# A gated attention kernel on one Trainium2 core: block order, tail priorities, filler matmuls and the last adds

## The chip, the core and the metric

The kernel runs on one core of one Trainium2 chip. A core has a matrix engine (TensorE, PE in the profile), a vector engine (VectorE, DVE), an engine for activation functions (ScalarE, ACT), a general engine (GpSimd, POOL) and a queue processor (SyncE, SP) that here only issues DMAs. They work on an on-chip memory (SBUF) and on a small memory for matmul results (PSUM, eight banks of 128 x 512 fp32). The engines run independently, each through its own list of instructions in order, and wait for each other with semaphores.

The metric is the time of one execution on the device in microseconds (us). Before the change the median of three runs is 483.76 us (483.73 to 483.79).

## What is computed

```
xn  = layernorm(x)                              # x: 2048 x 448
q, k, v = split(xn @ wqkv)                      # 16 heads of 28
o   = softmax(q k^T / sqrt(28)) v               # per head, 2048 x 2048 scores
s   = o @ wo
g   = silu(gelu(xn @ w1 + b1) @ w2 + b2)        # hidden size 1792
out = x + s * g
```

All tensors are bf16. The exponentials of the softmax, 16 x 2048 x 2048 of them, are the largest single piece of elementwise work.

## The kernel before

**Tiles and blocks.** The 16 heads form four groups g of four, since four heads of 28 (padded to 32) fill the 128 rows of the matrix engine. The 2048 queries form four chunks c of 512. A pair (g, c) is a block; there are 16. A block has 64 score tiles (16 key tiles x 4 heads), each 128 keys x 512 queries, one PSUM bank. All 1024 tiles are numbered m, and m // 64 is the block's number b. In the kernel before, g = b // 4 and c = b % 4: all chunks of a group are run before the next group, and the last four blocks are (3,0), (3,1), (3,2), (3,3).

**The stream.** Units of three tiles run through six PSUM banks, the ring: TensorE computes scores (`p_scores`, L1129), ScalarE takes the exponential of the unit into one of 21 SBUF slots P (`p_exps`, L1160), TensorE multiplies P by v (`p_pv`, L1346) and accumulates in one bank, `acc`. One column of v holds a constant, so that `acc` also holds the softmax's sums.

**Late tiles.** Some tiles are not given to ScalarE. VectorE copies the scores as integers out of the ring (L1183, L1274) and takes the exponential by a polynomial, one or two tiles at a time (`p_exp2`, L1297 to L1304). `pick_late` decides tile by tile, by VectorE's planned backlog against two values per block, THS and SLACKS.

**The end of a block.** VectorE copies `acc` to SBUF (E_sb, L1403), after which the next block's PV may begin. TensorE collects the sums (L1410), VectorE takes reciprocals (L1413), GpSimd splits them into two bf16 parts (L1415, L1416), TensorE spreads them (L1425), VectorE multiplies (L1432). The result overwrites this block's part of q.

**The last block** is cut by queries into pieces of 256, 128 and 128, so that its ends can overlap: E copies at L1377, sums spread by one matmul with `selb` (L1388), a reciprocal on 128 x 128 (L1391), and the product (L1394).

**Gate and output.** Between the score units the matrix engine computes the two layers of the gate branch: GELU on ScalarE in the middle of the run, the second layer at L1065, its bias at L1070, SiLU through a tanh on ScalarE (L1080) and VectorE (L1083). `p_out` and `p_last` make 128 x 448 output tiles: matmuls with wo (`t_wo`, L1442), times g (L1451), plus x (L1453), then a DMA from SP (L1459, for the last chunk L1457). A tile of chunk c needs all four groups of that chunk, and the gate of that chunk. For the very last tile (chunk 3, tile 3), tanh waits for the last exponential (L1093) and GpSimd forms g in two steps (L1095, L1097). While the blocks run, one PSUM bank (`misc`) is left for all of this; two ring banks' worth comes free with the last two exponentials.

**Who sets the order.** The program is planned as it is built. Every piece of work is a small process that hands out tasks with an engine, what they read and write, an estimated duration and a priority (a smaller number goes first). `run` repeatedly takes the task that can start first; among those of one engine that could start within 0.1 us of it, the one of the smallest priority. The order that comes out is fixed in each engine's instruction list. Estimated times never reach the chip; only order and waits do.

**Fillers.** [...]`p_busy` (L857) emits groups of three small matmuls of a zero matrix into `acc` (priority 95) whenever the planned busy share of the last 3.4 us is low (`pe_low`, from the history `pe_hist`). They add zero to `acc`, so they are ordered with its readers and writers.

## Time and profile before

| | |
|---|---|
| median of three runs | 483.76 us |
| the profiled execution, its own time | 484.9 us |
| its span, first to last instruction | 483.1 us |
| mean granted TensorE clock | 0.993 |
| exponentials on ScalarE (L1160) | 350 instructions: 249 of three tiles, 100 of two, 1 of one |
| late tiles on VectorE | 68 (L1183) and 8 (L1274) |
| starts of the 15 E copies (L1403) | 47.1 (block 0) ... 259.8, 315.2, 343.9, 371.6, 401.0, 424.3, 453.0 (block 14) |
| second gate layer's bias steps (L1070), last | 414.5 |
| output tiles' products (L1451) | 420.4 to 479.9 |
| last exponential ends | 476.46 |
| output DMAs, median from issue to landing | 1.9 us (six of 224 KB), 1.7 us (four of 112 KB) |

How to read it: shares and durations are of one execution. A line number names the line of the kernel, or of the helper, that issued the instruction. "Idle before" is the time in which an engine waited, with the instruction that ended the wait. In windows and the timeline, times count from the span's start. Between an engine's last instruction and the end of the span lies the last output DMA.

### The profile page before, as it was taken

To read this page: it belongs to the slowest core of one execution; us is meant where nothing else is said; L and a number is where in the kernel's file an instruction comes from. 1 tells how busy PE (TensorE), PEld (TensorE's weight loads), DVE (VectorE), ACT (ScalarE), POOL (GpSimd) and SP (SyncE) were. 2 spreads that over 40 slices of the span, in tenths; PEclk is the share of its full clock that TensorE was granted. 3 is DMA by queue.
4 is the path that set the end of the run, shared out by engine and by line. 5 is a ranking of instruction groups with operands and counts; after the bars stand their busy time and mean duration, and the time that the engine had idled before them with its cause. 6 is when DMAs were issued, how large, how long until landed. Compare 5 with 4: busy or idle time off the path is not lost.

```text
span 483.1 us, 10155 instructions
## 1 busy us (share of the span) xinstructions
PE 438.5 (91%) x4232; PEld 168.1 (35%) x4268; DVE 407.6 (84%) x592; ACT 468.8 (97%) x390; POOL 43.2 (9%) x77
## 2 busy tenths in 40 slices
PE   6999899998889898999989988999999999999995
PEld 5442333332223333332323343333333333333453
DVE  8946888989978989989878749899997999889785
ACT  5999999999999999999999999999999999999994
POOL 7470000000010000000101000010100100100001
PEclk9998999999999999999999999999999999999998
DMA  8501000000000000000400000000101010011011
GB/s 247 149 9 28 1 0 2 1 2 2 0 1 1 1 1 1 1 2 1 134 1 0 1 2 0 1 2 1 38 1 40 1 38 1 23 37 58 3 39 39
DMA packets 8288, 11.08 MB, mean 23 GB/s; under 512 B 1650, under 2 KB 6898, under 8 KB 8243
## 3 DMA queue, kind: packets, MB, share of 16 engines
q1 hardware_dynamic: 8098, 10.21, 7.0%
q8 instruction: 33, 0.54, 0.5%
q10 hardware_dynamic: 144, 0.23, 0.1%
q14 instruction: 13, 0.10, 0.1%
HBM read 8.61 MB, written 1.84 MB: 22 GB/s over the span
## 4 chain that ended last, share of the span: by engine, by line
ACT 45%; PE 32%; issue 17%; DVE 5%; ACTq 0%; DVEq 0%
ACT P L1160 42%; PE ring L1129 9%; PE acc L1346 6%; PE misc L1065 4%; PE acc L857 3%; PE misc L695 2%; ACT h L1044 2%; PE misc L1007 1%; PE acc L839 1%; PE misc L949 1%; PE misc L1442 1%; PE ring L1007 1%; ACT w L1080 1%; PE ring L949 1%; DVE kT L1298 0%
## 5 line engine op out<-in xcount | busy, mean ns | idle before, releaser
L1160 ACT ACTIVATE P<-ring 128x1536 bf16<-128x1536 f32 (+1 forms) x350 | 428.9, 1469 | 1.7 <-PE ring L1129 1.5
L1129 PE MATMUL ring<-qT,kT 32*128 32x512 bf16 (+2 forms) x1144 | 136.5, 360 | 26.1 <-ACT P L1160 22.0
L1346 PE MATMUL acc<-P,vaug 128*32 128x512 bf16 (+2 forms) x1074 | 95.0, 363 | 1.0 <-issue 0.5
L1129 PEld LDWEIGHTS ring<-qT,kT 32*128 32x128 bf16 x1144 | 35.5, 91 | 132.8 <-ACT P L1160 123.5
L1183 DVE TENSOR_SCALAR x_sb<-ring 128x512 int32<-128x512 f32 x68 | 46.8, 688 | 14.2 <-PE ring L1129 13.0
L1065 PE MATMUL misc<-w,h 128*128 128x448 bf16 x224 | 52.3, 355 | 0.1
L1415 POOL CAST rhi<-rc 128x16 bf16<-128x16 f32 x15 | 10.3, 686 | 402.5 <-DVE rc L1413 255.6
L857 PE MATMUL acc<-ident,zero 128*128 128x128 bf16 x516 | 44.8, 221 | 0.0
L1346 PEld LDWEIGHTS acc<-P,vaug 128*32 128x32 bf16 x1074 | 24.4, 93 | 51.0 <-issue 46.6
L857 PEld LDWEIGHTS acc<-ident,zero 128*128 128x128 bf16 x516 | 29.8, 98 | 21.3 <-issue 19.4
L1007 PE MATMUL misc<-xnT,w 128*128 128x512 bf16 x127 | 35.9, 382 | 1.3 <-issue 0.8
L990 DVE CAST h<-misc 128x512 bf16<-128x512 f32 x35 | 24.1, 688 | 8.1 <-PE misc L1007 7.0
L1304 DVE SCALAR_TENSOR_TENSOR x_sb<-x_sb,kT 128x1024 uint16<-128x1024 int32 (+1 forms) x24 | 26.7, 1111 | 0.5
L1302 DVE SCALAR_TENSOR_TENSOR kT<-kT 128x1024 f32<-128x1024 f32 (+1 forms) x24 | 26.6, 1110 | 0.5
L1298 DVE SCALAR_TENSOR_TENSOR kT<-kT 128x1024 f32<-128x1024 f32 (+1 forms) x24 | 26.5, 1104 | 0.6
L1300 DVE SCALAR_TENSOR_TENSOR kT<-kT 128x1024 f32<-128x1024 f32 (+1 forms) x24 | 26.4, 1102 | 0.2
L1065 PEld LDWEIGHTS misc<-w,h 128*128 128x128 bf16 x224 | 17.3, 97 | 23.9 <-issue 12.1
L1007 PE MATMUL ring<-xnT,w 128*128 128x512 bf16 x82 | 19.3, 380 | 2.0 <-ACT h L1044 1.6
L1298 DVE SCALAR_TENSOR_TENSOR w<-w 128x1024 f32<-128x1024 f32 (+1 forms) x18 | 20.3, 1128 | 0.3
L1304 DVE SCALAR_TENSOR_TENSOR x_sb<-x_sb,w 128x1024 uint16<-128x1024 int32 (+1 forms) x18 | 20.3, 1130 | 0.2
L1300 DVE SCALAR_TENSOR_TENSOR w<-w 128x1024 f32<-128x1024 f32 (+1 forms) x18 | 20.3, 1130 | 0.2
L1302 DVE SCALAR_TENSOR_TENSOR w<-w 128x1024 f32<-128x1024 f32 (+1 forms) x18 | 20.3, 1129 | 0.1
(154 smaller groups left out, 449.6 us busy)
## 6 DMA issues: line engine op xcount, KB each, us to landing
h<-in_A_x_dram SPq DMA_DIRECT2D x4, 448.0 KB, 3.3
w<-in_B_w_dram SPq DMA_DIRECT2D x1, 1568.0 KB, 7.3
x_sb<-in_A_x_dram SPq DMA_DIRECT2D x3, 448.0 KB, 5.2
w<-in_B_w_dram SPq DMA_DIRECT2D x1, 1344.0 KB, 9.4
out_dram<-h SPq DMA_DIRECT2D x6, 224.0 KB, 1.9
h<-in_A_wqkv_dram SPq DMA_DIRECT2D x3, 168.0 KB, 5.5
out_dram<-h SPq DMA_DIRECT2D x4, 112.0 KB, 1.7
wo<-in_A_wo_dram SPq DMA_DIRECT2D x16, 24.5 KB
```

What stands on the lines that cost most here:

```text
L857: ins = eng.matmul(K.acc[:, 0:128], K.zero[:, :], K.ident[:, :], start=False, stop=True, skip_group_check=True)
L990: yield _Task(DVE, lambda eng: eng.tensor_copy(dst, bank), [tok], wr, 0.69, 0.0, 2)
L1007: ins = eng.matmul(bank, K.w1[:, kt, ft * 128:(ft + 1) * 128], K.xnT[:, kt, c * 512:(c + 1) * 512], start=(kt == 0), stop=(kt == KT - 1))
L1065: ins = eng.matmul(ps, hv[:, ft, t * 128:(t + 1) * 128], K.w2[:, ft, :], start=(ft == 0), stop=(ft == FT - 1))
L1129: return eng.matmul(K.ring[:, RB[m], col:col + nq], K.kT[32 * j:32 * j + 32, g, t * 128:(t + 1) * 128], K.qT[32 * j:32 * j + 32, g, c * 51 ...
L1160: return eng.activation(K.P[:, p0:p0 + n, :], K.ring[:, b0:b0 + n, :], ACTF.Exp, scale=SM_SCALE)
L1183: yield _Task(DVE, lambda eng, m=m, i=i, half=half: eng.tensor_scalar(K.ysb[i][:, 512 * half:512 * half + 512], K.ring[:, RB[m], :], SM_SC ...
L1298: yield _Task(DVE, lambda eng: eng.scalar_tensor_tensor(u, v, EXP_A, v, op0=ALU.add, op1=ALU.mult), [tv], [tu], d1, 0.0, 4)
L1300: yield _Task(DVE, lambda eng: eng.scalar_tensor_tensor(u, u, EXP_B, u, op0=ALU.add, op1=ALU.mult), [tu], [tu], d1, 0.0, 4)
L1302: yield _Task(DVE, lambda eng: eng.scalar_tensor_tensor(u, v, EXP_D, u, op0=ALU.mult, op1=ALU.add), [tv, tu], [tu], d1, 0.0, 4)
L1304: yield _Task(DVE, lambda eng: eng.scalar_tensor_tensor(pl.bitcast(dt.uint16), y, 2.0 ** -9, u, op0=ALU.mult, op1=ALU.add), ty + [tu], [K. ...
L1346: return eng.matmul(K.acc[32 * j:32 * j + 32, q0:q0 + nq], K.vaug[:, t, 4 * g + j, :], ap[:, col:col + nq], tile_position=(0, 32 * j), sta ...
```

## The change

- **Block order.** A table GC gives (g, c) for each block number. The first eleven are as before; then come (3,0), (3,1), (3,2), (2,3), (3,3). So the last two blocks both belong to chunk 3, and chunks 0 to 2 have all four groups one block earlier.
- **Late-tile values.** THS changes for blocks 11 (8 to 7), 13 (8 to 4) and 14 (7 to 9), SLACKS for block 8 (3 to 2).
- **No fillers ahead of a PV copy.** A flag `hold` is set when a block's last PV matmuls have been planned and cleared when the E copy has been; while it is set, tasks of priority 90 or more on TensorE are no candidates.
- **The history of activity** counts the sums' small matmuls (L877, L1410) with a weight of 0.15 or 0.3.
- **Look-ahead in the end.** From the last 18 tiles on, TensorE and VectorE give up the chosen task for one of smaller priority number that can start before the chosen one would have ended less 0.1 us.
- **Priorities in the end.** The last tile's steps get priority 0 (1 for its last wo matmul), and tiles 0 to 2 of the last chunk a 2 for the `selb` matmul. The first three wo matmuls of a last-chunk tile become three tasks.
- **x added by GpSimd.** The adds of L1453 move to GpSimd for output tiles 8 to 13 of 16 (all of chunk 2, tiles 0 and 1 of chunk 3).
- **The last gate tile.** Its add (L1097) moves from GpSimd to VectorE.

```diff
+GC = [(b // C, b % C) for b in range(11)] + [(3, 0), (3, 1), (3, 2), (2, 3), (3, 3)]
...
-THS = (8.0, 4.0, 7.0, 8.0, 4.0, 7.0, 9.0, 6.0, 6.0, 8.0, 8.0, 8.0, 8.0, 8.0, 7.0, 3.0)
-SLACKS = (6.0, 5.0, 3.0, 5.0, 2.0, 6.5, 9.0, 6.5, 3.0, 4.0, 7.0, 6.0, 8.0, 6.0, 8.0, 3.0)
+THS = (8.0, 4.0, 7.0, 8.0, 4.0, 7.0, 9.0, 6.0, 6.0, 8.0, 8.0, 7.0, 8.0, 4.0, 9.0, 3.0)
+SLACKS = (6.0, 5.0, 3.0, 5.0, 2.0, 6.5, 9.0, 6.5, 2.0, 4.0, 7.0, 6.0, 8.0, 6.0, 8.0, 3.0)
...
+TAIL = 18
+POOL_ADD = 8
...
-            self.pe_hist.append((start, start + t.dur))
+            self.pe_hist.append((start, start + t.dur * t.w))
...
-                    if s is not None:
+                    if s is not None and not (self.hold and p[3].E == PE and p[3].prio >= 90):
                         cand.append((s, p))
...
+            if self.exp_m >= MTOT - TAIL and E in (PE, DVE):
+                for s2, p2 in sorted(((c[0], c[1]) for c in cand), key=lambda c: c[0]):
+                    if p2[3].E == E and p2[3].prio < p[3].prio and s2 < s + p[3].dur - 0.1:
+                        s, p = s2, p2
+                        break
...
             yield _Task(ACT, lambda eng: eng.activation(sg[:, 3, :], fb[:, 3, :], ACTF.Tanh, scale=0.5),
-                        [K.b_fsb[c % 2]], [K.b_sig3], 0.47, 0.0, 0)
+                        [K.b_fsb[c % 2]], [K.b_sig3], 0.87, 0.0, 0)
             yield _Task(POOL, lambda eng: eng.tensor_tensor(o, sg[:, 3, :], fb[:, 3, :], ALU.mult),
-                        [K.b_sig3, K.b_fsb[c % 2]], [K.b_h[c], K.b_g3], 0.85, 0.05, 0)
-            yield _Task(POOL, lambda eng: eng.tensor_tensor(o, o, fb[:, 3, :], ALU.add),
-                        [K.b_fsb[c % 2]], [K.b_h[c], K.b_g3], 0.85, 0.05, 0)
+                        [K.b_sig3, K.b_fsb[c % 2]], [K.b_h[c], K.b_g3m], 1.03, 0.05, 0)
+            yield _Task(DVE, lambda eng: eng.tensor_tensor(o, o, fb[:, 3, :], ALU.add),
+                        [K.b_fsb[c % 2], K.b_g3m], [K.b_h[c], K.b_g3], 0.4, 0.0, 0)
...
             if end:
+                K.hold = True
                 K.spawn(K.p_epi(b) if b < NBLK - 1 else K.p_epi4(first - NBLK + 1), 0.5)
...
         K.E_done = NBLK - 1 + s
+        K.hold = False
...
-        yield _Task(DVE, lambda eng: eng.tensor_tensor(o, o, K.x2[:, c, t, :], ALU.add),
-                    [K.b_x2[c], wr], [wr], 0.4, 0.0, 3)
+        E, dur = (POOL, 1.05) if POOL_ADD <= 4 * c + t < 14 else (DVE, 0.4)
+        yield _Task(E, lambda eng: eng.tensor_tensor(o, o, K.x2[:, c, t, :], ALU.add),
+                    [K.b_x2[c], wr], [wr], dur, 0.0, pr)
...
-        bank, tok = yield ("bank", lambda: K.on_done[(G - 1) * C + c] and K.g_done[c])
+        bank, tok = yield ("bank", lambda: K.on_done[GC.index((G - 1, c))] and K.g_done[c])
...
-        yield K.t_wo(ps, tok, c, t, (0, 1, 2), 3)
+        for g in range(G - 1):
+            yield K.t_wo(ps, tok, c, t, (g,), 3)
         yield ("until", lambda: K.on4[t])
-        yield K.t_wo(ps, tok, c, t, (3,), 3)
+        yield K.t_wo(ps, tok, c, t, (3,), 3 if t < 3 else 1)
```

Left out: the same lookup of (g, c) in `p_scores`, `p_mlate`, `p_pv` and `p_epi`, the new field w of a task, and the priorities named above.

## The prediction

> **What bounds the kernel now.** I read the page first (engine shares, costliest groups), then the chain of work in order of time, the waits, a table of windows by block, and last the timeline of the end.
>
> The page:
>
> ```profile
> PE 438.5 (91%) x4232; PEld 168.1 (35%) x4268; DVE 407.6 (84%) x592; ACT 468.8 (97%) x390; POOL 43.2 (9%) x77
> ...
> L1160 ACT ACTIVATE P<-ring 128x1536 bf16<-128x1536 f32 (+1 forms) x350 | 428.9, 1469 | 1.7 <-PE ring L1129 1.5
> ...
> L1183 DVE TENSOR_SCALAR x_sb<-ring 128x512 int32<-128x512 f32 x68 | 46.8, 688 | 14.2 <-PE ring L1129 13.0
> ```
>
> ScalarE is the bound: the softmax exponentials (L1160) run almost without a gap. The 68 tiles of L1183, and 8 more of L1274, are the "late" ones that VectorE exponentiates. What a tile costs ScalarE is read from the chain in order of time (start, length, what):
>
> ```profile
> 367.67 0.82 ACT P L1160
> 368.58 1.10 ACT P L1160
> 369.91 2.53 ACT P L1160 x2
> ```
>
> An instruction of two tiles holds ScalarE 0.91 us (to 368.58), one of three 1.33 (to 369.91): 0.42 per tile. One more late tile is worth 0.42 us as long as VectorE can pay for it. Against 0.91 and 1.33, the excess spacing over all exponentials after the first block is about 4.2 us, about 2.0 of that within half a microsecond of a block's end.
>
> The table of windows for the last two blocks and the end:
>
> ```profile
> core 0: us, PE busy (x) PEld busy (x) DVE busy (x) ACT busy (x) POOL busy (x), PEclk, DMA share, GB/s
> ...
> 424.30:453.00 28.70, 26.65 (x301) 11.52 (x304) 24.02 (x36) 28.70 (x24) 0.41 (x2) 1.00 0.10 34
> 453.00:476.50 23.50, 21.81 (x458) 11.72 (x452) 18.41 (x34) 23.50 (x20) 0.95 (x2) 1.00 0.08 27
> 476.50:483.10 6.60, 1.89 (x24) 0.73 (x22) 3.86 (x8) 0.42 (x1) 2.06 (x2) 0.77 0.16 52
> ```
>
> ScalarE is full until the last exponential, then 6.6 us follow in which one chain runs. VectorE is idle for 4.7 us of block 14 and 5.1 of block 15. The waits name one item that the change addresses, the copy of the PV bank (total, times, longest):
>
> ```profile
> DVE E_sb L1403 <- PE acc L857: 4.1, 5, 2.1
> ```
>
> **What the Trainium skill says.** (1) SBUF — State Buffer, "Who interferes with whom": a VectorE instruction with two SBUF inputs contends with a GpSimd instruction that reads SBUF, and "the second one to issue" (its summary's words) blocks until the first ends. The trace agrees both ways:
>
> ```profile
> 237.20 1.18 DVE L1298 SCALAR_TENSOR_TENSOR kT<-kT 128x1024 f32<-128x1024 f32 x1
> ...
> 237.35 1.08 POOL L1415 CAST rhi<-rc 128x16 bf16<-128x16 f32 x1 [23.19 <-DVE rc L1413]
> ...
> 156.34 0.20 POOL L1415 CAST rhi<-rc 128x16 bf16<-128x16 f32 x1 [21.90 <-DVE rc L1413]
> ```
>
> A GpSimd cast of 0.20 us takes 1.08 beside a VectorE step of a late tile and ends 0.05 after it. In the other direction, VectorE's L657 at 6.9 us took 1.00 us instead of 0.38 while GpSimd's L726 (6.78 to 7.78) ran. (2) TensorE: Matmul & The Clock Gate, "Architectural detail": VectorE's queue is strictly in order, so what stands behind a waiting copy waits too; the trace shows VectorE idle for up to 2.1 us before L1403. (3) The same page, Part 1: the clock falls only after about 3.4 us of low activity. The trace shows 1.00 in the blocks and 0.77 in the end stretch; holding fillers back for half a microsecond should not lower it.
>
> **The change part by part.**
>
> *No filler ahead of the PV copy.* Block 14's last PV matmuls end at 452.51, fillers (L857) on the same bank run to 452.96, the copy starts at 452.99: 0.42 us late. Block ends read in this way give 0.53, 0.53, 0.40, 0.25 and 0.42, 2.1 us in all, and nothing at the other ten. PE's next PV and its sums wait for that copy; ScalarE does not, since the 21 P slots (seven exponentials of three) cover it. So the gain is VectorE time, 1.07 us in the last three blocks. If fillers were needed for the clock, the loss would show as PEclk under 1.00. Weighting the tiny matmuls in the filler history adds fillers of 0.17 us; I cost them at nothing because PE waits for ScalarE 123.5 us in all at L1129.
>
> *The block order.* (3,2) now ends as block 13 (424.3), not 14 (453.0), so chunk 2's four output tiles are released some 29 us earlier. In the trace they lie at 458.8 to 467.5, between the steps of block 15's two late tiles: 4 x (0.62 + 0.39) = 4.05 us of VectorE. The late result that PV of block 15's first half waits for ends at 465.2. One more late tile alone costs 0.69 + 0.41 + 4 x 0.69 = 3.86 us, so the freed time pays for one: -0.42. Group 3's projections, wanted a block earlier, end at 311.3, before block 11 starts (343.9): no cost. The four tiles go into block 14 behind those of chunks 0 and 1 (they last ran 437.0 to 444.9, 2.4 us apart, so to about 455): 4 x 0.62 = 2.5 us of L1451 there at most; its 4.7 us of idle covers that. Their two output DMAs move with them on SP's queue, which then holds nothing else; they land in 1.9 us.
>
> *Thresholds.* A lower value of block 13 (8 to 4) admits fewer late tiles, a higher one of block 14 (7 to 9) more; blocks 8 and 11 move by one. No row prices this: between two tiles fewer and two more, +0.85 to -0.85.
>
> *x added by GpSimd.* Six adds of 0.39 leave VectorE, four of them (1.56 us) in block 14; the last two are in the end stretch, where VectorE has room. GpSimd takes 1.03 us for this shape (L1097) and is otherwise idle there. But the adds have two SBUF inputs, and so have the four steps of a late tile: each can hold VectorE up for 0 to 1.03 us. Four adds give back 1.56 and cost 0 to 4.1; I take half, 2.1, so half a microsecond net loss to VectorE, and +0.15 us for ScalarE where a late copy (L1183) is delayed and its ring bank comes free late (bounds 0 and +1.9).
>
> *One more late tile from the rest.* VectorE gets back 1.07 (holds) + 1.56 (adds) in blocks 12 to 14, against 3.47 per tile in a pair (0.69 + half of 0.69 + 4 x 1.22). That is 0.76 of a tile: -0.32.
>
> *Block-end gaps of ScalarE.* 2.0 us now, mostly a late copy and an E copy close together. An earlier E copy and changed late positions may mend or make such gaps: -0.6 to +0.6, I take -0.25.
>
> *The end.*
>
> ```profile
> 477.16 0.29 DVE L1377 CAST E_sb<-acc 128x128 bf16<-128x128 f32 x1 [0.27 <-PE acc L1346]
> 477.44 0.63 DVE L1451 TENSOR_TENSOR h<-ring,h 128x448 bf16<-128x448 f32 x1
> ...
> 477.81 0.22 PE L1388 MATMUL ring<-E_sb,selb 128*128 128x128 bf16 x1
> 478.06 0.96 DVE L1391 RECIPROCAL w<-ring 128x128 f32<-128x128 f32 x1
> 478.11 1.03 POOL L1097 TENSOR_TENSOR h<-h,w 128x448 bf16<-128x448 bf16 x1
> 479.13 0.29 DVE L1394 TENSOR_TENSOR qT<-E_sb,w 128x128 bf16<-128x128 bf16 x1
> ```
>
> The sum matmul L1388 stands behind output matmuls on PE, and the reciprocal behind tile 2's L1451 on VectorE. In the undisturbed case of 467.18 the reciprocal starts 0.33 us after the copy's end (467.51); here 0.61 (477.45 to 478.06). Priority and look-ahead can give back 0.28. The GpSimd add L1097 becomes a VectorE add of 0.39, which has its place in the 0.46 us between L1394 and L1451 (479.42 to 479.88), where tile 2's add is now. So tile 2's two instructions must go earlier or come last: bounds -0.35 and +0.73 (1.01 - 0.28). I take -0.28, since without chunk 2's work block 15's first half, and with it tiles 0 to 2, can be over earlier.
>
> Sum: -0.42 - 0.32 - 0.25 + 0.15 - 0.28 = -1.1 us. Of the profiled execution (484.9, its span 483.1 and 1.8 around it) that makes 483.8. It stands 1.1 above the median of 483.76, and the same step from the median gives 482.6.
>
> **Rivals.** *A late tile gained and one lost*: block 14 is fuller by up to 2.5 us, block 13 admits fewer, so the count stays at 68, and the tail and half a gap remain: -0.4, 483.3. For it: the last blocks' VectorE idle time is only 4.7 and 5.1 us. Against it: block 15's room is freed where a late tile can use it.
>
> *Slower, the shared port*: in block 14 VectorE is busy 24.0, plus 2.5 of moved work, minus 0 (those adds were not there before), plus up to 4.1 of blocking: 30.6 us in a block of 28.7. From 2.2 us of blocking on (4.7 - 2.5) VectorE overruns, late copies hold ring banks, and ScalarE waits for PE. At the full 4.1 that is +1.9; with a late tile's worth lost too and the tail gained, 483.76 + 1.9 - 0.28 = 485.4 at most, and some 485.1 typically. For it: the two lock cases above. Against it: L1451 comes straight before each add, and VectorE's next step starts within 0.04 us, ahead of GpSimd, which then waits.
>
> *Tile 2 last*: the look-ahead prefers everything of tile 3, and tile 2's L1451 and L1453 close the kernel: +0.73 at the end, minus one late tile: 484.1.
>
> **How the numbers follow.** 0.2% is 0.97 us, about what a measurement can tell: faster is under 482.79, slower over 484.73. The main case, 482.6 (its own range 481.2 to 482.8: two late tiles more below, half the tail gain missing above), gets 0.54; the unchanged count 0.22, all within the bound; tile 2 last 0.10, of it 0.03 slower; the port 0.14, of it 0.13 slower. So faster 0.54, same 0.30, slower 0.16. The range 481.2 to 484.4 leaves out the port case and a twentieth below.
>
> **What would show it.** L1160's tiles fewer by one or two and the late copies 69 or 70; chunk 2's L1451 before 456 us; no filler between the last PV and the E copy; the reciprocal 0.33 us after the last copy; about 6.3 us after the last exponential. Wrong would be: late copies at 68 or fewer, VectorE steps of late tiles lengthened by GpSimd's adds, ScalarE waiting for PE L1129 for more than the present 1.5 us, or tile 2's add as the last instruction.

## The result, and the profile after

The changed kernel takes 486.71 us (median of four runs, 485.87 to 487.63) against 483.75 (483.66 to 483.79) before: a ratio of 1.0062, 95% interval 1.0044 to 1.008. It is slower by 3.0 us and lies outside the predicted range, which ended at 484.4.

The page of the changed kernel: engine shares, and the groups that answer to L1160 and L1183 of before (now L1169 and L1192), with TensorE's P times v (L1355):

```profile
PE 438.1 (90%) x4223; PEld 168.0 (35%) x4259; DVE 403.3 (83%) x576; ACT 469.7 (97%) x390; POOL 49.1 (10%) x82
...
L1169 ACT ACTIVATE P<-ring 128x1536 bf16<-128x1536 f32 (+1 forms) x350 | 429.6, 1465 | 3.1 <-PE ring L1138 2.7
...
L1355 PE MATMUL acc<-P,vaug 128*32 128x512 bf16 (+2 forms) x1075 | 95.0, 363 | 3.0 <-DVE x_sb L1313 1.8
...
L1192 DVE TENSOR_SCALAR x_sb<-ring 128x512 int32<-128x512 f32 x67 | 46.1, 688 | 13.4 <-PE ring L1138 12.5
```

ScalarE is still the bound, but three things differ: one late tile fewer (67, was 68), ScalarE waits 2.7 us for scores (1.5 before), and a new wait stands before L1355: TensorE waits 1.8 us for the last step of a late tile (L1313). The table of windows around the end of block 14 and for the end stretch:

```profile
core 0: us, PE busy (x) PEld busy (x) DVE busy (x) ACT busy (x) POOL busy (x), PEclk, DMA share, GB/s
...
452.00:455.00 3.00, 1.20 (x18) 0.41 (x22) 2.44 (x4) 1.74 (x3) 0.00 (x0) 1.00 0.23 82
455.00:458.00 3.00, 3.00 (x53) 1.45 (x57) 0.86 (x2) 2.93 (x3) 0.41 (x2) 0.65 0.00 0
458.00:461.00 3.00, 3.00 (x70) 1.66 (x60) 2.86 (x5) 2.08 (x3) 0.00 (x0) 0.78 0.01 3
```

In the first window TensorE (PE) works 1.20 of 3 us and ScalarE 1.74; in the next two TensorE is full, but at 0.65 and 0.78 of its clock, and ScalarE loses time again in the third. Most of the loss sits in these nine microseconds, of which ScalarE idles 2.25; the end stretch itself became shorter (6.14 us from the last exponential's end, 6.61 before).

**Where the time went.** The exponentials run back to back, so I count their *excess*: the spacing of two starts less 0.90 us after an instruction of two tiles and less 1.33 after one of three, summed by block. One tile moved to or from ScalarE counts 0.43 (1.33 less 0.90). Against before:

| term | us |
|---|---|
| one late tile fewer (67 against 68) | +0.43 |
| excess in block 14: 2.00 against 0.02 | +1.98 |
| excess in block 15: 1.26 against 0.26 | +1.00 |
| excess in block 12: 0.56 against 0.15 | +0.41 |
| excess in block 11 | -0.27 |
| end stretch: 6.14 against 6.61 | -0.47 |
| sum | +3.08 |

The medians differ by 2.96. The profiled execution of before holds 1.25 us in its first block that no other profile but that of e11 holds, with the clock at 0.65 from 42 to 46 us. It is left out of the table. Because of it the two spans (483.08 and 484.89) differ by only 1.81, less than the medians.

### The profile page after: what moved, and what is told of

Same layout as the page of the kernel before. It is cut to its first block, busy times and chain, and to the rows that moved or that the text cites. A ratio compares the mean times of both kernels' runs of the same rounds, so it can differ in the third digit from the quotient of the medians.

```text
span 484.9 us, 10132 instructions
## 1 busy us (share of the span) xinstructions
PE 438.1 (90%) x4223; PEld 168.0 (35%) x4259; DVE 403.3 (83%) x576; ACT 469.7 (97%) x390; POOL 49.1 (10%) x82
## 4 chain that ended last, share of the span: by engine, by line
ACT 42%; PE 31%; issue 17%; DVE 8%; DMA 1%; POOL 0%; ACTq 0%; DVEq 0%; POOLq 0%
ACT P L1169 39%; PE ring L1138 9%; PE misc L1074 6%; PE acc L1355 6%; PE acc L866 2%; ACT h L1053 2%; PE misc L1016 1%; PE misc L704 1%; ACT w L1089 1%; DVE x_sb L1313 1%; DVE st L632 1%; PE misc L1454 1%; PE misc L958 1%; PE ring L1016 1%; DVE kT L1311 1%
## 5 line engine op out<-in xcount | busy, mean ns | idle before, releaser
L1169 ACT ACTIVATE P<-ring 128x1536 bf16<-128x1536 f32 (+1 forms) x350 | 429.6, 1465 | 3.1 <-PE ring L1138 2.7
L1138 PE MATMUL ring<-qT,kT 32*128 32x512 bf16 (+2 forms) x1144 | 136.6, 361 | 26.2 <-ACT P L1169 22.5
L1355 PE MATMUL acc<-P,vaug 128*32 128x512 bf16 (+2 forms) x1075 | 95.0, 363 | 3.0 <-DVE x_sb L1313 1.8
L1138 PEld LDWEIGHTS ring<-qT,kT 32*128 32x128 bf16 x1144 | 35.5, 91 | 133.1 <-ACT P L1169 120.6
L1192 DVE TENSOR_SCALAR x_sb<-ring 128x512 int32<-128x512 f32 x67 | 46.1, 688 | 13.4 <-PE ring L1138 12.5
L1355 PEld LDWEIGHTS acc<-P,vaug 128*32 128x32 bf16 x1075 | 24.4, 94 | 51.5 <-issue 44.6
L1311 DVE SCALAR_TENSOR_TENSOR kT<-kT 128x1024 f32<-128x1024 f32 (+1 forms) x22 | 26.5, 1204 | 0.4
L1309 DVE SCALAR_TENSOR_TENSOR kT<-kT 128x1024 f32<-128x1024 f32 (+1 forms) x22 | 26.4, 1200 | 0.3
L1307 DVE SCALAR_TENSOR_TENSOR kT<-kT 128x1024 f32<-128x1024 f32 (+1 forms) x22 | 25.6, 1165 | 0.5
L1313 DVE SCALAR_TENSOR_TENSOR x_sb<-x_sb,kT 128x1024 uint16<-128x1024 int32 (+1 forms) x22 | 25.7, 1168 | 0.3
L1307 DVE SCALAR_TENSOR_TENSOR w<-w 128x1024 f32<-128x1024 f32 (+1 forms) x18 | 20.3, 1128 | 0.3
L1313 DVE SCALAR_TENSOR_TENSOR x_sb<-x_sb,w 128x1024 uint16<-128x1024 int32 (+1 forms) x18 | 20.3, 1130 | 0.2
L1309 DVE SCALAR_TENSOR_TENSOR w<-w 128x1024 f32<-128x1024 f32 (+1 forms) x18 | 20.3, 1129 | 0.2
L1311 DVE SCALAR_TENSOR_TENSOR w<-w 128x1024 f32<-128x1024 f32 (+1 forms) x18 | 20.3, 1128 | 0.1
```

The lines of the kernel that those rows point to most:

```text
L1138: return eng.matmul(K.ring[:, RB[m], col:col + nq], K.kT[32 * j:32 * j + 32, g, t * 128:(t + 1) * 128], K.qT[32 * j:32 * j + 32, g, c * 51 ...
L1169: return eng.activation(K.P[:, p0:p0 + n, :], K.ring[:, b0:b0 + n, :], ACTF.Exp, scale=SM_SCALE)
L1192: yield _Task(DVE, lambda eng, m=m, i=i, half=half: eng.tensor_scalar(K.ysb[i][:, 512 * half:512 * half + 512], K.ring[:, RB[m], :], SM_SC ...
L1307: yield _Task(DVE, lambda eng: eng.scalar_tensor_tensor(u, v, EXP_A, v, op0=ALU.add, op1=ALU.mult), [tv], [tu], d1, 0.0, 4)
L1309: yield _Task(DVE, lambda eng: eng.scalar_tensor_tensor(u, u, EXP_B, u, op0=ALU.add, op1=ALU.mult), [tu], [tu], d1, 0.0, 4)
L1311: yield _Task(DVE, lambda eng: eng.scalar_tensor_tensor(u, v, EXP_D, u, op0=ALU.mult, op1=ALU.add), [tv, tu], [tu], d1, 0.0, 4)
```

## The experiments

The theory from the two traces: the four GpSimd adds of chunk 2 (L1467) lie in block 14, lock VectorE's second input out, the last late tile comes late, and TensorE, in order, waits for it. A rival: the block order and the new values themselves fill block 14 too much, and the adds matter little. The hold and the tail are taken apart as well.

### The adds by GpSimd

**e1: the same instruction order, four adds cut short.** The adds of chunk 2 on GpSimd work on 8 of 448 columns; x is left out of the other 440 columns of these four output tiles.

```diff
-        yield _Task(E, lambda eng: eng.tensor_tensor(o, o, K.x2[:, c, t, :], ALU.add),
+        yield _Task(E, lambda eng: eng.tensor_tensor(o[:, 0:8 if E == POOL and c == 2 else D], o[:, 0:8 if E == POOL and c == 2 else D], K.x2[:, c, t, 0:8 if E == POOL and c == 2 else D], ALU.add),
```

> The changed kernel with every instruction in its place, but the four GpSimd adds of chunk 2 (L1467) add only 8 of 448 columns (x is left out of the rest of chunk 2's output). Theory 'port': the adds of 1.03 us held the port that VectorE's steps of a late tile need (three steps longer by 0.72, 0.84 and 0.72 us in the profile of after), so with short adds these steps are back at 1.22, 0.41 and 0.69 us, ScalarE's excess spacing in block 14 and at the start of block 15 falls from 3.2 us to under 1, and the time is 483.5 to 484.5 us with a spread of under 0.3. Theory 'order': block 14 is simply too full and a late tile is missing, whoever adds; the time stays above 485.5.

Measured: 484.01 us (483.80 to 484.30), ratio to before 1.0003 (0.9994 to 1.0011): inside the range expected of 'port', with a spread of 0.5 where under 0.3 was expected. With the order of instructions, late tiles and fillers as in the changed kernel, the work of the four adds alone costs 486.71 - 484.01 = 2.70 us, nearly the whole loss. This is a difference of medians, one of them over four runs that lie 1.8 us apart; the fastest of these is still 1.57 us above the slowest of e1. The timelines show how. VectorE in the changed kernel:

```profile
442.60 0.62 DVE L1464 TENSOR_TENSOR h<-misc,h 128x448 bf16<-128x448 f32 x1 [0.99 <-POOL h L1467]
443.14 1.21 DVE L1309 SCALAR_TENSOR_TENSOR kT<-kT 128x1024 f32<-128x1024 f32 x1
444.38 1.94 DVE L1311 SCALAR_TENSOR_TENSOR kT<-kT 128x1024 f32<-128x1024 f32 x1
...
447.91 1.25 DVE L1306 TENSOR_SCALAR kT<-x_sb 128x512 f32<-128x512 uint16 x1
...
450.33 1.41 DVE L1309 SCALAR_TENSOR_TENSOR kT<-kT 128x512 f32<-128x512 f32 x1
...
452.50 0.69 DVE L1313 SCALAR_TENSOR_TENSOR x_sb<-x_sb,kT 128x512 uint16<-128x512 int32 x1
```

GpSimd beside it:

```profile
440.62 1.88 POOL L1467 TENSOR_TENSOR h<-h 128x448 bf16<-128x448 bf16 x1 [9.39 <-DVE h L1464]
443.30 1.94 POOL L1467 TENSOR_TENSOR h<-h 128x448 bf16<-128x448 bf16 x1 [0.81 <-DVE h L1464]
446.93 1.94 POOL L1467 TENSOR_TENSOR h<-h 128x448 bf16<-128x448 bf16 x1 [1.70 <-DVE h L1464]
449.78 1.41 POOL L1467 TENSOR_TENSOR h<-h 128x448 bf16<-128x448 bf16 x1 [0.90 <-PE acc L866]
```

And VectorE in e1, the same steps:

```profile
443.47 1.23 DVE L1311 SCALAR_TENSOR_TENSOR kT<-kT 128x1024 f32<-128x1024 f32 x1
...
446.28 0.42 DVE L1306 TENSOR_SCALAR kT<-x_sb 128x512 f32<-128x512 uint16 x1
...
448.31 0.69 DVE L1309 SCALAR_TENSOR_TENSOR kT<-kT 128x512 f32<-128x512 f32 x1
...
449.76 0.69 DVE L1313 SCALAR_TENSOR_TENSOR x_sb<-x_sb,kT 128x512 uint16<-128x512 int32 x1
```

Read one pair: GpSimd's add is issued at 443.30, while VectorE's L1309 runs (443.14 to 444.35). The add does not end until 0.89 us after L1309, so GpSimd waited for it. VectorE's next step L1311 is issued at 444.38, 0.03 us later, and yet GpSimd goes first: its add ends at 445.24, and L1311 takes 1.94 instead of 1.23. So each meeting costs VectorE most of an add. L1311, L1306 and L1309 are longer by 0.71, 0.83 and 0.72, together 2.3 us. To this comes a plain wait: tile t+1's product (L1464 at 442.60) waits 0.99 us for tile t's add, since two tiles share one output buffer. The last late result of block 14 ends at 453.19 instead of 450.45.

The Trainium skill (SBUF — State Buffer, "Who interferes with whom") says that a VectorE instruction with two SBUF inputs contends with a GpSimd instruction that reads SBUF, and lists `tensor_scalar` among those that can contend as well; the trace agrees on both (L1309 and L1311, and L1306, which is a tensor_scalar with one tensor input: 1.25 against 0.42). The words on "the second one to issue" that the prediction quotes from the same page fit as well: the add was issued at 443.30 and L1311 at 444.38, so L1311 is the second to issue, and it is the one that waits. What I had made of it, that VectorE's next step would be ahead of a waiting GpSimd, the trace refutes.

Who waits for that result: TensorE in the changed kernel, and ScalarE behind it:

```profile
453.33 0.40 PE L1355 MATMUL acc<-P,vaug 128*32 128x512 bf16 x4 [1.81 <-DVE x_sb L1313]
...
454.10 0.39 PE L1138 MATMUL ring<-qT,kT 32*128 32x256 bf16 x6
...
456.74 0.61 PE L1138 MATMUL ring<-qT,kT 32*128 32x256 bf16 x6
...
458.69 0.61 PE L1138 MATMUL ring<-qT,kT 32*128 32x256 bf16 x6
```

```profile
454.54 3.88 ACT L1169 ACTIVATE P<-ring 128x1536 bf16<-128x1536 f32 x3 [1.26 <-PE ring L1138]
459.34 1.45 ACT L1169 ACTIVATE P<-ring 128x1536 bf16<-128x1536 f32 x1 [0.92 <-PE ring L1138]
```

Block 14's last P times v (L1355 at 453.33) needs the late tile, so TensorE stands 1.81 us; the score units L1138 are queued behind it and ScalarE runs dry for 1.26. From 455.9 us on the granted clock is low (0.65 in the window from 455), the same six score matmuls take 0.61 instead of 0.39, and ScalarE runs dry a second time for 0.92. In e1 the windows of the same place show neither:

```profile
452.00:455.00 3.00, 2.45 (x47) 1.13 (x47) 1.10 (x3) 3.00 (x4) 0.41 (x2) 1.00 0.00 0
455.00:458.00 3.00, 2.89 (x74) 1.60 (x72) 2.89 (x4) 3.00 (x4) 0.00 (x0) 1.00 0.01 3
```

**e2: all x adds on VectorE.**

```diff
-POOL_ADD = 8
+POOL_ADD = 99
```

> The changed kernel with all x adds on VectorE, so that the plan is made anew (66 late copies where after has 67 by L1192). Theory 'port': no lengthened step, excess in blocks 14 and 15 under 1 us; one more tile on ScalarE costs 0.43; some 484.2 us. Theory 'order': VectorE has 1.6 us more to do in block 14, so it is slower than after: over 486.7 us.

Measured: 484.44 us (484.25 to 485.15), ratio 1.0016 (1.0009 to 1.0022); 66 late tiles; excess of block 14 0.21, of block 15 0.05. Without the GpSimd adds the two stalls are gone, but the four adds on VectorE cost a late tile against e1. Moving them off VectorE thus has the gain that the plan sees, 0.43 us, and the cost of 2.70 that it does not see.

**e10: more of the adds on GpSimd** (tiles 4 to 13, ten instead of six).

```diff
-POOL_ADD = 8
+POOL_ADD = 4
```

> The changed kernel with x added by GpSimd for tiles 4 to 13 instead of 8 to 13, so chunk 1's four adds too, in blocks 13 and 14. Theory 'port': four adds more among late tiles' steps, each with up to 1.03 us of blocking; if they cost what the first four did (2.7 us), 488 to 490 us, if some fall beside other work, 487.3 at least. Rival: the first four hurt only because block 14 was full when they came; then the further ones change little: 486.3 to 487.2 us.

Measured: 484.81 us (484.51 to 486.17), ratio 1.0022 (1.0015 to 1.003). Both expectations missed: with more adds it is 1.9 us faster than the changed kernel. The trace has the same three steps lengthened (1.93, 1.25, 1.40), and two more (1.78, 1.45). But VectorE, which no longer does chunk 1's adds either, comes to the same steps earlier (L1311 at 442.04 instead of 444.38), and the last late result of block 14 ends at 450.84, near e1's 450.45. TensorE's pause there is 0.85 us, and its clock stays up:

```profile
452.00:455.00 3.00, 2.53 (x68) 1.31 (x66) 1.32 (x3) 2.44 (x3) 0.41 (x2) 1.00 0.02 5
```

ScalarE has one stall there (0.75 us at 452.2). So the price is not so much per add: three steps lengthened by the same amounts cost far less here. It depends on whether the delay reaches the last late tile that the block's P times v needs, and on whether the clock falls as well.

**e3: the GpSimd adds alone**, on the kernel before.

```diff
+POOL_ADD = 8
...
+        pr = 3
...
-        yield _Task(DVE, lambda eng: eng.tensor_tensor(o, o, K.x2[:, c, t, :], ALU.add),
-                    [K.b_x2[c], wr], [wr], 0.4, 0.0, 3)
+        E, dur = (POOL, 1.05) if POOL_ADD <= 4 * c + t < 14 else (DVE, 0.4)
+        yield _Task(E, lambda eng: eng.tensor_tensor(o, o, K.x2[:, c, t, :], ALU.add),
+                    [K.b_x2[c], wr], [wr], dur, 0.0, pr)
```

> The kernel before with one part of the change alone: x is added by GpSimd for tiles 8 to 13; block order, values, fillers and tail as before. Theory 'port': chunk 2's adds fall among block 15's two late tiles, some of their steps take 0.7 to 1 us longer, and PV of block 15's first half, which waits for the second of them, comes 1 to 2 us later; since ScalarE does not wait for that directly, the time is 484 to 486 us with a wider spread than before. Theory 'order': harmless, 483.0 to 483.8 us.

Measured: 484.25 us (484.06 to 486.01), ratio 1.0011 (1.0004 to 1.0018); 68 late tiles, excess by block as before (0.15, 0.04, 0.26), end stretch 7.11 instead of 6.61. The time is in the range expected of 'port', but not for its reason. In the old order chunk 2's adds lie in block 15. They lengthen two steps of its late tiles by 0.71 us each (L1307 and L1313, 1.40 instead of 0.69), and ScalarE loses nothing by it. The price of 0.50 is in the end stretch, where an add of GpSimd at 475.53 delays the gate's two GpSimd steps behind it, and the second of these (L1106, 477.63 to 478.66) holds VectorE:

```profile
478.02 0.79 DVE L1404 TENSOR_TENSOR qT<-E_sb,w 128x128 bf16<-128x128 bf16 x1
```

That product takes 0.29 us otherwise. The large loss needs the adds at the place that the new order and its values give them.

**e7: chunk 2's adds planned later.** In the changed kernel they become processes of their own that are planned only after block 15's first E copy. Nothing on the chip makes them wait for it.

```diff
+    def p_add(self, c, t, o, wr, pr):
+        K = self
+        yield ("until", lambda: K.E_done >= NBLK - 1)
+        yield from K.t_add(c, t, o, wr, pr)
```

> The changed kernel in full, but chunk 2's four GpSimd adds wait until the first E copy of the last block has been made, when no late tile is left on VectorE. Theory 'port': same work on the same engines, nothing to collide with: 483.8 to 484.3 us with a spread under 0.4, as with the short adds. Theory 'GpSimd adds as such' (their latency holds a buffer or an output DMA): over 485.5 us, as after.

Measured: 484.33 us (484.03 to 485.83), ratio 1.0016 (1.0009 to 1.0023), just over the range expected of 'port', and spread over 1.8 us instead of under 0.4. The adds did not wait as the expectation takes for granted. Excess of block 14 is 0.22, of block 15 still 0.78. GpSimd, with nothing left ahead of them in its list, ran the adds from 454.53 on, long before the E copy at 464.3, and lengthened the steps of block 15's late tiles:

```profile
454.53 5.44 POOL L1479 TENSOR_TENSOR h<-h 128x448 bf16<-128x448 bf16 x4
...
455.69 1.41 DVE L1306 TENSOR_SCALAR kT<-x_sb 128x1024 f32<-128x1024 uint16 x1
...
457.62 1.45 DVE L1307 SCALAR_TENSOR_TENSOR kT<-kT 128x1024 f32<-128x1024 f32 x1
459.11 1.94 DVE L1309 SCALAR_TENSOR_TENSOR kT<-kT 128x1024 f32<-128x1024 f32 x1
```

A later place in the plan is no delay on the chip where an engine's list is short. Still 2.4 us of the loss are recovered, with the same adds on the same engine: the place of the adds decides.

### Order, hold and tail

**e9: order, hold and new values, without the tail and the GpSimd adds.**

```diff
-POOL_ADD = 8
+POOL_ADD = 99
-            if self.exp_m >= MTOT - TAIL and E in (PE, DVE):
+            if self.exp_m >= MTOT and E in (PE, DVE):
...
-        for g in range(G - 1):
-            yield K.t_wo(ps, tok, c, t, (g,), 3)
+        yield K.t_wo(ps, tok, c, t, (0, 1, 2), 3)
```

The last gate step's split and the priorities of the end are those of the kernel before, too.

> The changed kernel without its tail part and without GpSimd adds: block order, values, hold and weights alone. Measured against the run with all x adds on VectorE (484.44, the same plus the tail), it prices the tail; against the run with the hold alone (484.12), it prices the block order. Theory 'the order costs, the tail gives': two late tiles fewer than before (66 copies, +0.85), a pair of stalls of 0.4 us in block 12, tail as before (6.6 us): 484.8 to 485.0 us. Theory of the prediction (the order frees VectorE in block 15 and is worth a late tile): under 483.8 us.

Measured: 484.83 us (484.43 to 485.42), ratio 1.0016 (1.0009 to 1.0023); 66 late tiles, end stretch 6.47, excess of block 12 0.56. So this part alone costs 1.1 us. Two late tiles account for 0.85 of it. The excess moves between blocks (+0.41 in block 12, -0.27 in block 11, +0.19 in block 14, -0.21 in block 15) and comes to about +0.1, and the end stretch gives back 0.14. That makes 0.83; the remaining 0.25 is not placed. From e9 to e2 only the tail is added: 484.83 to 484.44, a gain of 0.39.

**e5: the hold alone**, on the kernel before, with the weights in the filler history.

```diff
-                    if s is not None:
+                    if s is not None and not (self.hold and p[3].E == PE and p[3].prio >= 90):
...
-            self.pe_hist.append((start, start + t.dur))
+            self.pe_hist.append((start, start + t.dur * t.w))
```

> The kernel before with the hold and the history's weights alone. The plan has 67 tiles by L1192 or its counterpart instead of 68 (one fewer in block 15). Theory 'the hold buys nothing': the E copy is off ScalarE's path, so its earlier start changes no spacing, and the missing late tile costs 0.43 us: 484.1 to 484.3 us, tail after the last exponential as before (6.6). Theory of the prediction (VectorE time from the hold is worth a fraction of a late tile): under 483.7 us.

Measured: 484.12 us (483.84 to 484.45), ratio 1.0003 (0.9996 to 1.001). It has 67 late tiles and takes 0.37 us more, where one tile is 0.43; the interval includes no difference at all. Against e9 (484.83) the block order and its values cost 0.71.

**e6: the tail alone**, on the kernel before: the look-ahead, the priorities, the wo products one group at a time, the last gate step on VectorE.

```diff
+            if self.exp_m >= MTOT - TAIL and E in (PE, DVE):
+                for s2, p2 in sorted(((c[0], c[1]) for c in cand), key=lambda c: c[0]):
+                    if p2[3].E == E and p2[3].prio < p[3].prio and s2 < s + p[3].dur - 0.1:
+                        s, p = s2, p2
+                        break
```

> The kernel before with the changes of the tail alone (look-ahead, priorities, split matmuls, last gate add on VectorE); 68 late copies as before. Theory 'tile 2 last' (seen in the run with hold and tail, where the tail took 7.1 us): 484.2 to 484.4 us with tile 2's add as the last instruction. Theory of the prediction's main case: the reciprocal comes earlier, tail 6.3 us: 483.3 to 483.5 us.

Measured: 484.26 us (483.97 to 485.42), ratio 1.0011 (1.0003 to 1.002). The end stretch grew from 6.61 to 7.13, which is all of the loss. The tail's VectorE instructions say why:

```profile
478.63 0.39 DVE L1466 TENSOR_TENSOR h<-h 128x448 bf16<-128x448 bf16 x1
478.94 0.62 DVE L1463 TENSOR_TENSOR h<-ring,h 128x448 bf16<-128x448 f32 x1
479.59 0.39 DVE L1466 TENSOR_TENSOR h<-h 128x448 bf16<-128x448 bf16 x1
```

Tile 3's add (478.63) comes first, then tile 2's product and add close the kernel. That is my rival "tile 2 last", in the old order. The forecast +0.73 for it came out as +0.52.

**e4: hold and tail together**, on the kernel before (the edits of e5 and e6).

```diff
+            if self.exp_m >= MTOT - TAIL and E in (PE, DVE):
...
+                K.hold = True
```

> The kernel before with the hold, the weights of the history and all changes of the tail (look-ahead, priorities, split matmuls, the last gate add on VectorE), without the block order, the values and the GpSimd adds. Theory 'port': the rest of the change is sound, it gives the gain seen in block 0 (1.25 us of ScalarE's excess) and at the end (0.45) and loses one late tile (0.43): 482.5 to 483.2 us. Theory 'order' says the same of this run. If it is over 484 us, the tail or the hold have a loss of their own.

Measured: 484.67 us (484.45 to 485.2), ratio 1.0014 (1.0007 to 1.0021): 0.92 more than before, where e5 and e6 add up to 0.37 + 0.51 = 0.88. 67 late tiles and an end stretch of 7.13: the two effects add up. The expected 482.5 to 483.2 missed. It took the 1.25 us of block 0 for a gain of the change, but e3, e5 and e6 lack that excess too: it belongs to the profiled execution of before, in which the clock was low there.

### Versions that might beat both

**e8: order and fillers of before, the tail, chunk 2's adds planned late on GpSimd by e7's process**, and values set anew for blocks 10 to 15.

```diff
-THS = (8.0, 4.0, 7.0, 8.0, 4.0, 7.0, 9.0, 6.0, 6.0, 8.0, 8.0, 8.0, 8.0, 8.0, 7.0, 3.0)
-SLACKS = (6.0, 5.0, 3.0, 5.0, 2.0, 6.5, 9.0, 6.5, 3.0, 4.0, 7.0, 6.0, 8.0, 6.0, 8.0, 3.0)
+THS = (8.0, 4.0, 7.0, 8.0, 4.0, 7.0, 9.0, 6.0, 6.0, 8.0, 9.5, 10.0, 9.5, 7.0, 9.5, 5.0)
+SLACKS = (6.0, 5.0, 3.0, 5.0, 2.0, 6.5, 9.0, 6.5, 3.0, 4.0, 7.5, 9.0, 8.5, 5.0, 1.5, 0.0)
```

> A candidate for a version better than both: block order and fillers of before, the changed tail, the GpSimd adds deferred as in the run before this one, and late-tile values of blocks 10 to 15 set anew so that 68 late copies remain and tile 2 is done before the last E copy. If the tail's gain of 0.45 us is real and the adds are harmless when deferred: 483.0 to 483.4 us. If a late tile's stall or tile 2 spoils it: 483.8 or more.

Measured: 483.58 us (483.31 to 484.81), ratio 0.9998 (0.999 to 1.0007): no clear difference from before. It lies between the two ranges expected. The end stretch is 6.14, but ScalarE has a stall of 0.48 in block 13 and one of 0.49 in block 14.

**e11: e8 with a real wait.** The adds of chunk 2 also read the first E copy of the last block, so that they can't run earlier.

```diff
-                    [K.b_x2[c], wr], [wr], dur, 0.0, pr)
+                    [K.b_x2[c], wr] + ([K.b_E4[0]] if E == POOL and c < C - 1 else []), [wr], dur, 0.0, pr)
```

> The candidate with the block order and fillers of before (483.58 us) again, but the deferred GpSimd adds now really wait for the first E copy of the last block (they read what it writes), where the profile of the last one showed one add still meeting a late tile's step. 68 late copies. Expected 483.2 to 483.6 us: the tail's 0.47 us less some stalls of about 0.5 us in blocks 13 and 14.

Measured: 483.41 us (483.31 to 485.13), ratio 0.9993 (0.9982 to 1.0003): unclear, at most two tenths of a per cent faster.

**e12: the whole change, with e7's process, the real wait of e11**, and with values for blocks 10 to 15 set anew for its own order.

```diff
-THS = (8.0, 4.0, 7.0, 8.0, 4.0, 7.0, 9.0, 6.0, 6.0, 8.0, 8.0, 7.0, 8.0, 4.0, 9.0, 3.0)
-SLACKS = (6.0, 5.0, 3.0, 5.0, 2.0, 6.5, 9.0, 6.5, 2.0, 4.0, 7.0, 6.0, 8.0, 6.0, 8.0, 3.0)
+THS = (8.0, 4.0, 7.0, 8.0, 4.0, 7.0, 9.0, 6.0, 6.0, 8.0, 7.0, 8.0, 7.5, 8.5, 7.0, 6.0)
+SLACKS = (6.0, 5.0, 3.0, 5.0, 2.0, 6.5, 9.0, 6.5, 2.0, 4.0, 8.0, 6.0, 9.0, 4.5, 6.5, 4.0)
...
+                    [K.b_x2[c], wr] + ([K.b_E4[0]] if E == POOL and c < C - 1 else []), [wr], dur, 0.0, pr)
```

> The whole change (order, hold, weights, tail) with the adds of chunk 2 waiting for the first E copy of the last block and late-tile values of blocks 10 to 15 set anew so that 68 late copies remain (after has 67). Theory 'port and one late tile are all that is wrong with the change': tail 6.1 us, excess as before: 483.2 to 483.5 us. If the stalls of block 12 (0.4 us) stay with the order: 483.6 to 483.9.

Measured: 483.22 us (482.94 to 483.83), ratio 0.9984 (0.9977 to 0.9991), below both kernels: 3.5 us under the changed one, 0.5 under the one before. Its page, and the same four adds where they now lie:

```profile
L1169 ACT ACTIVATE P<-ring 128x1536 bf16<-128x1536 f32 (+1 forms) x350 | 428.7, 1481 | 0.7 <-PE ring L1138 0.5
...
L1192 DVE TENSOR_SCALAR x_sb<-ring 128x512 int32<-128x512 f32 x68 | 46.8, 688 | 14.5 <-PE ring L1138 13.6
```

```profile
463.21 4.05 POOL L1479 TENSOR_TENSOR h<-h 128x448 bf16<-128x448 bf16 x4 [4.71 <-DVE E_sb L1387]
464.45 0.93 DVE L1405 TENSOR_TENSOR qT<-E_sb,w 128x128 bf16<-128x128 bf16 x1
466.28 1.13 DVE L1405 TENSOR_TENSOR qT<-E_sb,w 128x128 bf16<-128x128 bf16 x1
```

Four adds in 4.05 us, at their undisturbed 1.0 each; they still hold VectorE up (L1405 0.93 and 1.13 instead of 0.29), but nothing that ScalarE needs hangs on it. ScalarE waits 0.5 us for scores in all (2.7 in the changed kernel), and the late tiles are 68 again. The second of the two stalls that the other runs with the new order have around the end of block 11 (0.28 and 0.24 at 370.1 and 371.3 in e9) is gone: e12 has only the first, 0.26, as before has (0.28). So it does not belong to the block order alone; it went with the new values. How much of the 3.5 us is the wait and how much the values isn't separated here. For the adds alone, e1 gives 2.70.

### The path from before to after

| kernel | us | step | late tiles | end stretch | excess, blocks 12 / 14 / 15 |
|---|---|---|---|---|---|
| before | 483.75 | | 68 | 6.61 | 0.15 / 0.02 / 0.26 |
| e9: + order, hold, values | 484.83 | +1.08 | 66 | 6.47 | 0.56 / 0.21 / 0.05 |
| e2: + tail | 484.44 | -0.39 | 66 | 6.15 | 0.56 / 0.21 / 0.05 |
| e1: + adds off VectorE, not yet done by GpSimd | 484.01 | -0.43 | 67 | 6.13 | 0.56 / 0.21 / 0.01 |
| after: + GpSimd does them | 486.71 | +2.70 | 67 | 6.14 | 0.56 / 2.00 / 1.26 |

## Why the prediction was wrong

The forecast was 482.6 us, the result 486.71. By its own steps:

**x added by GpSimd (+0.15, bounds 0 and +1.9): this step failed, and it decides the result.** Measured +2.70 (e1 to after), above the upper bound. The size of the blocking was near what I took: 2.3 us in three lengthened steps, where I had 2.1. Three things were wrong around it. The idle time that was to absorb it (4.7 us in block 14) is not where the delay falls: what counts is when the last late result of the block is ready, and it became 2.7 us later. The place of the wait was wrong: not late copies holding ring banks, but TensorE at block 14's last P times v, with the scores queued behind it. And no term stood for a fall of TensorE's clock, which gave a second stall (0.92 us) after the first (1.26); that the pause brought the fall is likely from their order in time, but not shown (see "The clock").

**The rival "slower, the shared port"** (485.1, at most 485.4) had the right cause and side, not the place or the size. Its "at most" also names a lost late tile and leaves its 0.42 out of the sum; with it, it would be 485.8, still under the result. I gave it 0.14 since I argued that VectorE's next step, issued within 0.04 us, would be ahead of a waiting GpSimd. That argument was made without a case of it in the trace: both cases that I showed had one instruction already running.

**One more late tile from the order (-0.42), and 0.76 of a tile from the rest (-0.32): wrong sign.** The count went from 68 to 67 (+0.43), and to 66 without the GpSimd adds (e2, e9). The work moved as forecast: chunk 2's products now start at 439.86 to 449.08, before 456. And time is freed by the hold: waits ahead of the block-end copies fell from 6.1 to 4.2 us, and hardly any of it is for a filler any more. Before and after:

```profile
L1403 DVE CAST E_sb<-acc 128x512 bf16<-128x512 f32 x15 | 10.3, 689 | 6.1 <-PE acc L857 4.1 <-PE acc L1346 1.8
...
L1414 DVE CAST E_sb<-acc 128x512 bf16<-128x512 f32 x15 | 10.3, 687 | 4.2 <-PE acc L1355 3.9
```

But no one spends it. `pick_late` compares a planned backlog with fixed values, and with these the hold alone (e5) admits one tile fewer. With values set for the new order, e12 has 68 with the hold and the order. My step read a time budget where the code has a threshold. My "two fewer to two more" for the thresholds held the outcome; the credits beside it did not. One of them was also counted twice: the term on GpSimd sets the adds' 1.56 us against 2.1 of blocking and ends with a loss to VectorE, and this term then credits the same 1.56 in full, 0.45 of its 0.76 tile.

**Thresholds by block**: block 13 was to admit fewer, block 14 more. By the times of L1192 between the block-end copies, blocks 11 to 15 have 4, 5, 6, 4, 1 late tiles (5, 7, 3, 4, 2 before): block 13 admits more, block 14 as many, blocks 11, 12 and 15 fewer.

**Block-end gaps (-0.25)**: +0.41 in block 12, -0.27 in block 11, so about +0.1 outside blocks 14 and 15, within my bounds of 0.6 either way. Most of this is a shift: of the two stalls at 370.1 and 371.3 us the first is there before the change too, but in block 11. The second is in the runs with the new order and the change's own values, also without GpSimd adds, and not in e12, which has the order with other values. What exactly brings it was not tested.

**The end (-0.28, bounds -0.35 and +0.73): right in direction, too small.** Measured -0.39 (e9 to e2), and -0.47 for the whole end stretch, both a little beyond the bound. The reciprocal starts 0.32 us after the last copy's end (forecast 0.33), and tile 2 is done before tile 3:

```profile
478.94 0.39 DVE L1467 TENSOR_TENSOR h<-h 128x448 bf16<-128x448 bf16 x1
479.26 0.29 DVE L1387 CAST E_sb<-acc 128x128 bf16<-128x128 f32 x1
479.87 0.96 DVE L1402 RECIPROCAL w<-ring 128x128 f32<-128x128 f32 x1 [0.32 <-PE ring L1399]
480.93 0.29 DVE L1405 TENSOR_TENSOR qT<-E_sb,w 128x128 bf16<-128x128 bf16 x1
481.14 0.38 DVE L1106 TENSOR_TENSOR h<-h,w 128x448 bf16<-128x448 bf16 x1
481.68 0.62 DVE L1464 TENSOR_TENSOR h<-ring,h 128x448 bf16<-128x448 f32 x1 [0.16 <-PE ring L1454]
482.34 0.39 DVE L1467 TENSOR_TENSOR h<-h 128x448 bf16<-128x448 bf16 x1
```

The condition I put on it held as well: with chunk 2's work gone from block 15, tile 2 is early; in the old order (e6, e4) it is last and the tail costs +0.52. The new order is not the only way to it: e8 and e11 keep the old one, with chunk 2's adds on GpSimd and other values, and their end stretch is 6.14 as well.

**The clock.** I wrote that holding fillers back should not lower it, and that holds: e5, with the hold, and e6, without it, both show 1.00 from 10 to 476 us. Their means (0.998 and 1.000) differ by the end stretch alone. But I read "1.00 in the blocks" from the last two blocks, and put a low clock down to low activity. The same trace has it low in the first block, with TensorE busy for over nine tenths of the time (PE busy is the second number, the clock the third from the end):

```profile
38.00:42.00 4.00, 3.66 (x35) 1.43 (x36) 3.00 (x6) 3.99 (x5) 0.00 (x0) 1.00 0.23 56
42.00:46.00 4.00, 3.81 (x21) 0.78 (x19) 1.62 (x3) 3.85 (x4) 0.00 (x0) 0.65 0.02 4
```

No pause over 0.2 us stands before it, and e6 has 1.00 in the same window with 3.64 of 4 us busy. The matmuls show the difference: two of a projection take 1.03 us at 43.2 here (L695) and 0.60 at 43.0 in e6 (L704). So a pause is not needed for a fall, and that the 1.81 us in block 14 brought the fall after it is not shown. The times of the changed kernel's four runs go with their mean clock: 485.87 at 0.997, 486.68 and 486.73 at 0.995, 487.63 at 0.991. How much of the 2.70 us is the clock's stays open: the trace puts 0.92 of ScalarE's waiting into the stretch of low clock and 1.26 before it, and no run has the pause with the clock known to stay up.

## What to carry to other kernels

Before elementwise work is moved to GpSimd beside a busy VectorE, look for the result on VectorE's chain that an in-order TensorE waits for next: four adds of 1.03 us cost 2.70 us ahead of it (a fall of the clock included), and in e12, behind it, nothing that could be seen. An instruction's place in a plan does not keep it from running early on an engine with a short list; only a dependency on the chip does. And time freed on an engine did not turn into a gain here while the rule that hands out work kept values that did not spend it (66 and 67 late tiles; 68 in e12): set its values anew together with the change.

## What the hardware showed that I had not expected

- A GpSimd add that waits for VectorE's running step gets the port ahead of VectorE's next step. That step was issued 0.03 us after the first one's end in two cases (1.23 became 1.94, 0.69 became 1.41) and just before it in the third (0.42 became 1.25).
- TensorE's clock fell some 2.5 us after the end of a pause of 1.81 us: 0.65 and 0.78 of full speed in the windows of 3 us from 455 and 458, in which TensorE was busy throughout. In e10, with a pause of 0.85 us (2.14 of 3 us busy from 449, then 2.53), it stayed at 1.00. In the profile of before it fell with no pause over 0.2 us. The Trainium skill (TensorE: Matmul & The Clock Gate, Part 1) ties the fall to an idle window of about 3.4 us; neither fall in the blocks had one, so here the measurement differs from the page.
- A low clock comes in some executions of a kernel and not in others. In e3, two of 18 runs have a mean of 0.993 and take 485.79 and 486.01 us; the other 16, at 0.997 to 0.999, take 484.06 to 484.37.
